# Two more tile pairs of a matrix product by seven products, two copies made independent, one load behind a wait, and a new order of all steps

## Chip, core and metric

The kernel runs on one core of a Trainium2 chip. The metric is the device time of one execution in microseconds; lower is better. The engines are TensorE (PE: matmuls and transposes into PSUM), VectorE (DVE) and ScalarE (ACT) for element-wise work, GpSimd (POOL), which here mostly issues the DMAs that convert float32 to float16, and SyncE (SP), which issues the other DMAs.

## What is computed

Local attention with eight global tokens, and then a low-rank mixer with a two-layer MLP. Shapes: q, k, v are 4 x 8 x 768 x 64 (batch, heads, tokens, head size), U is 768 x 32, V 32 x 768, w_ch1 512 x 2048, w_ch2 2048 x 512, all float32.

```python
scores = scale * np.matmul(q, k.transpose(0, 1, 3, 2))
keep = is_global | is_local            # key < 8, or 0 <= query - key < 96
scores = np.where(keep, scores + bias[None], -1e9)
a = np.exp(scores - np.max(scores, axis=-1, keepdims=True))
a = a / (np.sum(a, axis=-1, keepdims=True) + 1e-09)
x = np.matmul(a, v)                    # heads side by side: 4 x 768 x 512
h = x.transpose(0, 2, 1) @ U @ V
u = x + h.transpose(0, 2, 1)
out = u + np.maximum(u @ w_ch1, 0.0) @ w_ch2
```

## The kernel before

All arithmetic on TensorE is in float16 with float32 sums. The work is cut into small steps, each with a name, an engine and a Python function that issues its instructions. The list `ORDER` names all steps once. A planner walks through it, gives buffers and PSUM banks to the steps and a start time by its own estimates, and the program is issued in the order of these start times. So `ORDER` sets what each engine does after what; each engine works through its own instructions strictly in that order.

**Attention** goes by pairs of heads, 0 to 15, four pairs to a batch. A pair p has: loads of k, q and v (`lk`, `lq`, `lv`, by POOL, lines 457, 453 and 461; for pair 0, k and q come by SyncE in float32, line 471, and are cast by `Ck0`, `Cq0`); transposes of k and q on TensorE (`TK`, `TQ`) and copies out of PSUM (`EK`, `EQ`); a copy of the keys shifted by one block, with the global keys in its first 32 columns (`KO`, line 366 where SyncE makes it); the same for the values (below); scores (`S`, line 732, for batch 0 with a bias matmul `SB`, line 713), exponentials on ACT (`EX`, line 797), the mask product on DVE (`MK`), the product with the values (`PV`, lines 864 and 865), reciprocal and norm (`RC`, `NM`), a cast (`XC`), transposition and the product with U (`UP`, lines 838 and 843), copies and the product with V (`XE`, `XU`, `TE`, `HM`, line 964), and a copy of the result u into place (`E0`, `E1`). Which of ACT, DVE, SP or POOL makes a copy is a letter in a string of `CFG`, one letter for each pair: `KO`, `VO`, `XC`, `E`, `EK`, `EQ` and so on. `HR` says whether `HM` uses two groups of 64 rows (R) or all 128 rows (F).

**Shifted V.** `vo` holds V without its last block, and the global rows of V in its first 32 partitions for every block. `VC` copies all 128 partitions and `VG` then writes the 32 partitions over. With SyncE as their engine these are one DMA, a wait for its landing, and two more DMAs.

**MLP-1** (u @ w_ch1 with relu) has for each batch 16 tiles of 128 columns of w_ch1. An ordinary tile takes four 384-column matmuls for each half of the tokens, as one step with both halves (`M1a`, `M1b` and a relu `RL` of 768 columns, lines 1042 and 1060) or as two half tiles (line 1018, relus `RL` and `RM` of 384 columns, line 1024). `CFG["Z"]` names tile pairs (z and z + 8) of a batch that are computed together in the manner of Strassen and Winograd: seven products of two matmuls each (`ZP1` to `ZP7`, line 1113) in place of sixteen matmuls. They need sums of blocks of u (`ZT`, lines 1070 to 1073, once for a batch) and of w_ch1 (`ZS`, lines 1091 to 1094, kept in `zs` for pairs 4 to 7 and made in an `ep` buffer for others), copies of partial results out of PSUM on ACT (`ZU`, `ZW`, `ZX`), additions on DVE (`ZA`, `ZB`, `ZD`, line 1131) and relus (`ZR` on ACT, line 1164; `ZQ` and `ZV` on ACT, line 1170, or DVE, line 1172, by the strings `ZQ` and `ZR`).

**MLP-2** goes in three parts t of 128 + 128 tokens, all by seven products (`P1` to `P7`, eight matmuls each, line 1244) that need sums of the hidden values on DVE (`PA`, `PB`, lines 1197 to 1203) and of w_ch2 (`TWa`, `TWb`). A remainder step `RS` opens each part (line 1236) with products of `vs`. `DA` to `DG` add the products to the rows held in `x_sb` (lines 1256 and 1296), and `O` stores them (line 1311).

**Weights** come in four pieces each: `w1_0` to `w1_3` serve tile steps n = 0 to 3, 4 to 7, 8 to 11 and 12 to 15 of MLP-1 (the number after the dot in `M1a0.13` is n, the one before it the batch).

**The small V of the mixer** is loaded twice. POOL loads its two halves as float16 into `vs` (`vs0`, `vs1`); SyncE loads it whole in float32 into `vf`, a corner of `x_sb` (`mixl`, line 516), for `vs2`, the difference of the halves on DVE. The planner lets `mixl` depend on `back`, a memset of one element by DVE (line 532):

```python
uf = x_sb[1][:, 0, 0:NB * R].rearrange("p (c r) -> p c r", r=R)
vf = x_sb[1][0:R, 2:4].rearrange("p a b -> p (a b)")[:, 0:S]
```

The memset writes `uf`, the load writes `vf`, so nothing in the program makes the one wait for the other.

Of the kernel before, what the change touches and what calls it, by code (L numbers as in the profile page):

```python
# [32 lines left out]
M1a0.6 RL0.6 VC5 M1b0.7 MK5.0 M1a0.4 MK5.1 M1b0.10 RM0.10 TK6 EK6 KO6 VG5 M1b0.5 RM0.5 M1a0.0 M1c0.0 M1d0.0 M1b0.0  # L33
MK5.2 RM0.7 RL0.0 PA0.3 PV5 lq8 RL0.4 M1b0.8 RM0.8 lk8 mask6 M1a0.5 RL0.5 UP4 XE4 RC5 NM5 M1a0.12 lq9 PB0.3 XC5
M1a0.1 TWa0 M1a0.7 RL0.12 TWb0 M1b0.6 lv8 RM0.6 VC7 RL0.7 PA0.1 PB0.1 XU4 TE4 M1c0.1 lq10 M1d0.1 lk9 M1b0.1 RL0.1
PA0.0 lv6 M1a0.8 RL0.8 M1a0.9 lk10 RL0.9 M1b0.9 RM0.9 PB0.0 PA0.2 PB0.2 HM4 S7.0 EX7.0 MK7.0 RS0.0 E04 P20.0 TWa1
# [15 lines left out]
P61.1 TK14 EK14 DB1.0 P71.0 HM9 E09 DF1.1 RC11 NM11 DD1.0 S12.0 DC1.0 DB1.1 DC1.1 EX12.0 RS1.2 P11.2 P41.0 DA1.2
DG1.0 lk15 S12.1 EX12.2 P31.2 VC10 P71.1 VG10 EX12.1 MK10.0 MK10.2 PV10 TK13 EK13 KO13 MK12.0 XC11 UP11 DD1.1 RC10
KO14 XE11 NM10 XC10 P61.2 TQ13 EQ13 DB1.2 P21.2 DF1.2 UP10 XE10 P71.2 DD1.2 XU11 MK12.1 XU10 TE10 O1.3 P41.1 TE11
DG1.1 HM10 E010 S14.0 EX14.0 HM11 E011 E111 ZT2 P41.2 TD2 O1.1 ZP12.7 ZU2.7 S14.1 EX14.2 MK14.2 EX14.1 ZP12.6 ZU2.6
P51.2 DG1.2 DC1.2 O1.2 MK14.0 ZP22.7 TK15 M1b2.4 RM2.4 EK15 KO15 M1a2.1 TQ15 ZA2.7 ZP62.6 ZW2.6 M1b2.1 RL2.1 ZP62.7
ZW2.7 M1b2.5 ZP52.6 MK12.2 ZP72.6 EQ15 ZX2.6 ZB2.6 M1a2.5 RL2.5 ZP12.4 ZP42.6 ZR2.6 O1.5 M1a2.4 RL2.4 ZP32.6 M1a2.3
M1b2.3 ZD2.6 RM2.5 MK14.1 RL2.3 PV12 RC12 ZV2.6 ZP72.7 ZX2.7 ZP52.7 O1.4 O1.0 VG14 NM12 ZP22.6 M1a2.0 XC12 ZB2.7
M1b2.0 ZU2.4 ZV2.7 ZA2.6 ZP32.7 ZD2.7 RL2.0 PV14 ZP12.5 ZU2.5 RC14 NM14 PA2.0 ZP62.4 ZW2.4 UP12 ZP22.4 ZA2.4 ZP42.7
ZP62.5 XE12 ZW2.5 ZR2.7 ZP22.5 XU12 TE12 ZA2.5 M1a2.7 PB2.0 RL2.7 ZP72.4 ZP72.5 ZX2.5 ZP52.5 ZB2.5 HM12 ZV2.5 E012  # L60
ZP52.4 ZQ2.7 ZX2.4 M1a2.2 ZP42.5 ZR2.5 XC14 ZP32.5 UP14 XE14 ZB2.4 ZV2.4 ZP32.4 M1b2.2 RL2.2 ZD2.5 ZP42.4 ZR2.4 XU14
# [1335 lines left out]
```

## Time and profile before

| | us |
|---|---|
| median of 3 runs | 226.85 (224.6 to 227.18) |
| profiled execution | 227.05 |
| its span, first to last instruction | 225.3 |

The time of an execution is its span and 1.75 us around it. TensorE's granted clock is 1.00 all through. By stretch, from the profile's busy times (a stretch ends where TensorE begins the next kind of work, roughly):

| stretch (us) | what TensorE mainly does | PE busy | DVE busy | ACT busy | GB/s |
|---|---|---|---|---|---|
| 0 to 57.2 | attention and MLP-1 of batch 0 | 51.56 | 44.12 | 44.04 | 174 |
| 57.2 to 82 | MLP-2 of batch 0, attention of batch 1 | 24.80 | 20.80 | 15.98 | 140 |
| 82 to 109 | MLP-1 of batch 1 | 27.00 | 23.28 | 22.25 | 134 |
| 109 to 135 | MLP-2 of batch 1, attention of batch 2 | 26.00 | 21.60 | 16.36 | 60 |
| 160 to 182 | MLP-2 of batch 2, attention of batch 3 | 22.00 | 18.62 | 9.43 | 13 |
| 182 to 203 | MLP-1 of batch 3 | 21.00 | 16.57 | 15.55 | 76 |
| 203 to 225.2 | MLP-2 of batch 3, last stores | 18.92 | 16.03 | 1.36 | 73 |

Matmuls are pipelined: the busy time of a group of matmuls counts each from its start to its modelled end, and that is about twice the time after which the next one starts. What a matmul costs a full TensorE is read from the chain of waits, where several follow each other.

### The profile page before, as it was taken

Reading aid. Unit: us, or ns where it says so; the run is one execution under the profiler, and the core shown is the slowest. Engines: PE = TensorE matmul, PEld = TensorE weight load, DVE = VectorE, ACT = ScalarE, POOL = GpSimd, SP = SyncE. Lnnn points to the kernel's source line nnn. Section 1 sums busy time; section 2 is a strip of 40 time slices with the busy share of each in tenths; the row PEclk is TensorE's granted clock in tenths of the full one; section 3 lists DMA queues with packets and bytes.
Section 4 is the critical chain, followed back from the end, with each engine's and each line's share of the span. In section 5 each row is a group of like instructions: output and inputs, shape, how many; then the busy total and the mean of one; then the engine's idle time right before and its main releaser. Section 6 shows DMA issues by size and latency. Waiting matters only on the chain.

```text
span 225.3 us, 5972 instructions
## 1 busy us (share of the span) xinstructions
PE 216.3 (96%) x2422; PEld 157.7 (70%) x2422; DVE 181.5 (81%) x403; ACT 144.5 (64%) x257; POOL 72.5 (32%) x94
## 2 busy tenths in 40 slices
PE   7799889799999999999999999999999999999994
PEld 2556645566788976566788886666688876658883
DVE  5789847869978878788888879598987887979792
ACT  4898876688767659877665678778752357782000
POOL 8889956543794935010091000004000000000000
PEclk9999999999999999999999999999999999999999
DMA  6999999999999999874097501409200016000015
GB/s 173 172 167 141 178 181 177 188 196 167 160 130 127 144 151 219 151 121 80 8 95 48 129 2 51 145 4 102 70 11 3 0 49 235 1 0 4 23 57 202
DMA packets 87612, 24.01 MB, mean 107 GB/s; under 512 B 75840, under 2 KB 84736, under 8 KB 87584
## 3 DMA queue, kind: packets, MB, share of 16 engines
q0 software_dynamic: 71552, 13.93, 73.7%
q1 hardware_dynamic: 16032, 9.69, 15.4%
q8 instruction: 19, 0.31, 0.6%
q14 instruction: 9, 0.07, 0.1%
HBM read 27.56 MB, written 6.29 MB: 150 GB/s over the span
## 4 chain that ended last, share of the span: by engine, by line
PE 80%; DMA 15%; POOL 3%; issue 1%; ACT 0%; SPq 0%; DVE 0%; DVEq 0%; POOLq 0%
PE ps L1244 33%; PE ps L1113 14%; PE ps L1018 10%; DMA w<-in_moe_w_ch_dram 9%; PE ps L1042 7%; DMA vt<-in_v_dram 4%; PE ps L732 4%; PE ps L610 3%; PE ps L838 2%; DMA sA<-in_q_dram 2%; PE ps L865 2%; POOL stgq L457 2%; PE ps L864 1%; PE ps L964 1%; PE ps L1236 1%
## 5 line engine op out<-in xcount | busy, mean ns | idle before, releaser
L797 ACT ACTIVATE ep<-ps 128x1024 f16<-128x1024 f32 (+1 forms) x48 | 43.9, 951 | 16.0 <-PE ps L732 14.8
L1244 PEld LDWEIGHTS <-htr 128*128 128x128 f16 x392 | 36.3, 98 | 6.2 <-issue 2.2
L1018 PE MATMUL ps<-uT,w 128*128 128x384 f16 x176 | 33.2, 326 | 1.4 <-DMA w<-in_moe_w_ch_dram 1.4
L1256 DVE TENSOR_TENSOR x_sb<-x_sb,ps 128x256 f32<-128x256 f32 (+1 forms) x60 | 27.0, 466 | 9.3 <-PE ps L1244 9.0
L1244 PEld LDWEIGHTS <-sA 128*128 128x128 f16 x288 | 27.1, 98 | 4.1 <-issue 0.4
L1018 PEld LDWEIGHTS <-w 128*128 128x128 f16 x176 | 16.5, 98 | 12.2 <-DMA w<-in_moe_w_ch_dram 1.9
L1024 ACT ACTIVATE htr<-ps 128x384 f16<-128x384 f32 x44 | 20.4, 492 | 7.0 <-PE ps L1018 6.0
L1244 PE MATMUL ps<-w,sA 128*128 128x256 f16 x192 | 24.3, 273 | 0.0
L1244 PE MATMUL ps<-tB,htr 128*128 128x256 f16 (+1 forms) x200 | 23.9, 268 | 0.0
L457 POOL DMA_DIRECT2D stgq<-in_q_dram x24 | 20.2, 851 | 11.5 <-DMA w<-in_moe_w_ch_dram 5.8
L1244 PE MATMUL ps<-w,htr 128*128 128x256 f16 x192 | 23.8, 273 | 0.0
L457 POOL DMA_DIRECT2D stgk<-in_k_dram x24 | 20.3, 856 | 8.1 <-PE ps L610 5.2
L1042 PE MATMUL ps<-uT,w 128*128 128x384 f16 x112 | 21.3, 326 | 0.7 <-DMA w<-in_moe_w_ch_dram 0.7
L1131 DVE TENSOR_TENSOR htr<-ps,zu 128x384 f16<-128x384 f32 x30 | 16.5, 554 | 5.8 <-PE ps L1113 4.0
L461 POOL DMA_DIRECT2D vt<-in_v_dram x16 | 16.7, 1045 | 12.2 <-DMA vo<-vt 8.8
L810 DVE TENSOR_TENSOR ep<-ep,mask 128x1024 f16<-128x1024 f16 x24 | 16.2, 684 | 2.4 <-ACT ep L797 2.4
L362 ACT ACTIVATE zu<-ps 128x384 f32<-128x384 f32 x30 | 14.7, 495 | 5.0 <-PE ps L1113 4.0
L928 POOL DMA_DIRECT2D x<-x_sb x3 | 2.5, 823 | 46.2 <-DVE sA L1197 28.0
L1042 PEld LDWEIGHTS <-w 128*128 128x128 f16 x112 | 10.6, 98 | 7.5 <-DMA w<-in_moe_w_ch_dram 0.8
L903 DVE TENSOR_TENSOR x_sb<-ps,rcp 128x768 f32<-128x768 f32 x16 | 15.3, 957 | 0.5
L1113 PEld LDWEIGHTS <-w 128*128 128x128 f16 x108 | 10.1, 98 | 6.4 <-issue 0.2
L732 PE MATMUL ps<-qT,kT 64*128 64x128 f16 x192 | 14.1, 217 | 0.0
(125 smaller groups left out, 452.3 us busy)
## 6 DMA issues: line engine op xcount, KB each, us to landing
out_dram<-x_sb SPq DMA_DIRECT2D x22, 256.0 KB, 2.4
w<-in_moe_w_ch_dram POOLq DMA_DIRECT2D x8, 512.0 KB, 10.7
vt<-in_v_dram POOLq DMA_DIRECT2D x16, 192.0 KB, 6.4
stgk<-in_k_dram POOLq DMA_DIRECT2D x24, 96.0 KB, 5.8
stgq<-in_q_dram POOLq DMA_DIRECT2D x24, 96.0 KB, 5.7
...
```

Source lines behind the costliest of these rows:

```text
L457: nc.gpsimd.dma_start(o[:, i], src[b, h0 + i].rearrange("(n p) d -> p n d", p=P))
L461: nc.gpsimd.dma_start(vt[gv.slot][:, :, :, 0:D], v[b, h0:h0 + 2].rearrange("h (n p) d -> p h n d", p=P),)
L732: nc.tensor.matmul(t[:, hi, j * P:(j + 1) * P], lhs, qt[r, i * P:(i + 1) * P], start=not biased, stop=True, skip_group_check=biased,)
L797: nc.scalar.activation(ep[gep.slot][:, :, lo:512], ps[:, gsc.slot:gsc.slot + 2, lo:512], AF.Exp, scale=qk_scale)
L810: nc.vector.tensor_tensor(ev, ev, mv, ALU.mult)
L1018: nc.tensor.matmul(ps[:, g.slot, 0:HS], w1[:, dc, jt * P:(jt + 1) * P], ub[:, dc, i * HS:(i + 1) * HS], start=(dc == 0), stop=(dc == NDC - 1),
L1024: nc.scalar.activation(htr[:, jt, i * HS:(i + 1) * HS], ps[:, g.slot, 0:HS], AF.Relu)
L1042: nc.tensor.matmul(ps[:, g.slot + half, 0:HS], w1[:, dc, jt * P:(jt + 1) * P], ub[:, dc, half * HS:(half + 1) * HS], start=(dc == flat[0]) ...
L1113: nc.tensor.matmul(bank(g), a()[:, i], bq[:, i], start=first and i == 0, stop=last and i == 1, skip_group_check=True,)
L1131: return lambda: nc.vector.tensor_tensor(o, x(), y(), ALU.add)
L1244: nc.tensor.matmul(o if part is None else o[:, part], a[:, j, c0 + cols.start:c0 + cols.stop], bq[:, j] if part is None else bq[:, j, part ...
L1256: nc.vector.tensor_tensor(o, o, x, ALU.add)
```

## The change

- `Z` names pairs 2 and 3 for batch 2 too: six pairs instead of four there (batch 1 has four, batch 3 six), sixteen in all. Four ordinary tiles of batch 2 go (`M1` n = 2, 3, 6 and 7). The sums `ZS2.2` and `ZS2.3` are made in `ep` buffers.
- `VC` on SyncE copies partitions 32 to 127 only. `VG` then no longer waits for it; both wait for the load of V alone, and the product with the values waits for both.
- The memset `back` writes an element of `vf`. The load `mixl` writes the same place, and so is issued behind the memset.
- The four stores of rows 0 to 511 of batch 0 are split into halves by columns (`OS`).
- Many letters of the engine strings change, `HR` of pairs 2 and 3 from R to F, and the planner's size for `u16`.
- `ORDER` is new from end to end. Shown are its beginning before and after, up to the last piece of w_ch2, and the part around MLP-1 of batch 2 after.

```diff
-ones3 wz lk0 iota ones0 lk1 lq0 lq1 vz lk3 relf rel3 bias1 bias0 bias2 SB0.0 bias4 Ck0.1 Ck0.0 lv0 ones1 Cq0.0 vs1
-TK0 EK0.1 lk2 SB0.1 lq2 mask2 Cq0.1 EK0.0 TQ0 ones2 SB0.2 mask0 lq3 EQ0.0 lv1 EQ0.1 KO0.1 KO0.0 TK1 EK1 S0.2 TQ1 EQ1
-mask7 EX0.2 KO1 VC0 VG0 S0.0 EX0.0 S0.1 back EX0.1 TK3 EK3 SB1.2 KO3 lk4 u16 vs0 lv2 S1.2 EX1.2 SB1.1 S1.1 EX1.1 PV0
-RC0 NM0 TK2 EK2 SB2.2 KO2 XC0 TQ2 EQ2 VC1 VG1 lk5 SB1.0 S1.0 EX1.0 lv3 lq4 lq5 w1_0 w1_3 lk7 w1_2 SB2.1 S2.1 TQ3
-S2.2 EQ3 lq7 PV1 RC1 NM1 EX2.1 lv4 EX2.2 SB3.1 S3.1 EX3.1 UP0 XE0 SB2.0 mask1 XC1 S2.0 XU0 TE0 EX2.0 VC2 TK4 EK4 VG2
-SB3.0 S3.0 EX3.0 TK5 EK5 VC3 VG3 HM0 E00 SB3.2 S3.2 PV2 RC2 NM2 XC2 EX3.2 UP1 XE1 TQ4 PV3.0 PV3.1 PV3.2 RC3.2 EQ4
-lq6 w1_1 RC3.0 NH3.0 RC3.1 NH3.1 NH3.2 NM3 KO4 mixl XU1 lk6 TE1 lv5 TQ5 EQ5 UP2 XE2 HM1 E01 UP3.0 XU2 TE2 UP3.1
-UP3.2 XE3 HM2 XU3 E02 M1a0.3 M1c0.3 TE3 HM3 E13 E03 S4.1 KO5 EX4.2 w2_0 MK4.2 M1d0.3 M1b0.3 RL0.3 M1b0.13 EX4.1
-M1a0.14 MK4.1 RL0.14 TK7 M1a0.13 EK7 M1b0.14 ZS6 KO7 M1a0.2 RM0.14 M1c0.2 M1d0.2 TD0 M1b0.2 M1b0.15 TQ7 EQ7 RL0.13
-ZS5 VC4 VG4 RL0.2 RM0.15 S4.0 EX4.0 MK4.0 S5.0 EX5.0 M1a0.15 ZS7 M1a0.10 RL0.10 M1a0.11 RL0.11 M1b0.12 RL0.15
-M1b0.11 RM0.12 w2_2 RM0.13 RM0.11 TQ6 EQ6 w2_3 lv7 vs2 PV4 RC4 NM4 M1b0.4 mask3 XC4 RM0.4 w2_1 S5.1 EX5.1 EX5.2
...
+ones0 wz iota lk0 lq0 lk1 lq1 vz vs1 relf rel3 bias0 bias1 SB0.2 Ck0.0 lk3 SB0.1 lq2 Ck0.1 lv0 TK0 bias2 bias4 mask2
+mask1 lk2 Cq0.0 Cq0.1 TQ0 SB0.0 mask3 EQ0.0 EK0.0 KO0.0 EK0.1 KO0.1 lq3 ones1 ones3 lv1 EQ0.1 S0.0 TK1 EK1 KO1 ones2
+EX0.0 S0.2 EX0.2 S0.1 TQ1 EQ1 u16 lk5 mask0 SB1.2 TK3 EK3 KO3 lq5 VC0 VG0 lv2 EX0.1 lv3 vs0 SB1.1 w1_0 S1.2 EX1.2
+lk4 S1.1 EX1.1 TQ2 EQ2 lq4 SB1.0 S1.0 TK2 EK2 KO2 PV0 RC0 EX1.0 VC1 VG1 NM0 XC0 TQ3 lq7 w1_3 lk7 w1_2 EQ3 SB2.0
+SB2.2 S2.2 EX2.2 S2.0 EX2.0 PV1 RC1 NM1 XC1 SB2.1 S2.1 EX2.1 SB3.0 S3.0 EX3.0 UP0 XE0 VC2 VG2 VC3 SB3.1 S3.1 EX3.1
+XU0 TE0 VG3 SB3.2 lv5 S3.2 EX3.2 PV2 RC2 NM2 XC2 TK5 EK5 HM0 E00 lk6 PV3.0 PV3.1 PV3.2 RC3.1 RC3.0 NH3.0 UP1 XE1 UP2
+XE2 TQ5 RC3.2 EQ5 NH3.1 XU1 TE1 TK4 EK4 XU2 TE2 NH3.2 HM1 E01 UP3.0 UP3.1 UP3.2 XE3 NM3 HM2 E02 lv4 back mixl TQ4
+EQ4 w1_1 XU3 TE3 KO4 M1a0.3 TQ7 EQ7 M1c0.3 HM3 E03 KO5 E13 M1d0.3 S4.1 EX4.2 lq6 M1b0.3 RL0.3 M1b0.13 RM0.13 MK4.2
+M1b0.14 RM0.14 M1b0.15 RM0.15 EX4.1 TK7 EK7 KO7 M1b0.12 RM0.12 M1a0.15 ZS7 RL0.15 M1a0.13 M1a0.11 M1a0.2 w2_1 RL0.11
+S5.0 EX5.0 S4.0 ZS5 MK4.1 VC5 VG5 EX4.0 MK5.0 M1c0.2 w2_3 M1b0.9 M1a0.14 RL0.14 M1a0.12 ZS6 RL0.13 RM0.9 TD0 TK6 EK6
+M1d0.2 M1b0.2 RL0.2 M1a0.8 RL0.8 RL0.12 vs2 M1b0.11 RM0.11 VC4 VG4 w2_2 S5.1 EX5.1 M1b0.10 RM0.10 M1b0.5 EX5.2
+M1b0.6 RM0.6 w2_0 MK4.0 PV4 TQ6 RM0.5 M1a0.10 RL0.10 MK5.1 lk9 EQ6 M1a0.7 RC4 NM4 lq8 M1b0.7 RM0.7 KO6 M1a0.6 M1b0.4
...
+NM10 ZS2.2 P41.1 DG1.1 XC10 P21.2 UP10 XE11 XU11 P31.2 MK12.1 ZS2.3 XE10 XU10 TE10 ZP12.3 TE11 TQ13 ZU2.3 VC14 O1.4
+HM10 E010 TD2 DF1.2 HM11 P71.2 E111 O1.3 EQ13 VG14 S14.0 TK15 E011 EX14.0 O1.1 DD1.2 ZP12.2 ZU2.2 P51.2 P41.2 ZP22.3
+ZT2 EK15 DC1.2 DG1.2 ZA2.3 ZP62.2 ZW2.2 ZP62.3 ZW2.3 O1.2 ZP22.2 ZA2.2 MK12.2 TQ15 ZP72.2 ZX2.2 ZP72.3 ZX2.3 ZP52.2
+ZB2.2 ZV2.2 EQ15 O1.5 ZP52.3 ZB2.3 ZP42.2 ZR2.2 ZP42.3 ZR2.3 ZP32.2 ZD2.2 ZQ2.2 PV12 RC12 NM12 ZP32.3 ZD2.3 MK14.0
+S14.1 EX14.2 MK14.2 EX14.1 M1a2.5 ZP12.4 ZU2.4 MK14.1 ZQ2.3 ZP22.5 ZP12.5 ZU2.5 ZA2.5 M1a2.1 RL2.5 M1b2.1 RL2.1
+ZP62.4 PV14 ZV2.3 RC14 ZP62.5 NM14 ZW2.5 M1b2.5 ZP22.4 ZP72.5 XC12 UP12 ZP52.5 ZA2.4 ZP12.6 RM2.5 XE12 XU12 ZX2.5
+PA2.1 TE12 M1a2.4 ZP42.5 ZB2.5 ZV2.5 HM12 E012 ZU2.6 ZP62.6 ZW2.4 ZP72.4 ZR2.5 ZX2.4 RL2.4 ZP32.5 ZD2.5 ZW2.6 ZP22.6
+ZA2.6 ZP52.4 ZP52.6 ZB2.4 ZV2.4 ZP42.4 ZR2.4 ZQ2.5 ZP12.7 ZP72.6 ZP22.7 ZU2.7 XC14 ZA2.7 ZX2.6 ZB2.6 lv15 VG15
+ZP32.4 ZD2.4 UP14 ZP62.7 M1b2.4 KO15 XE14 XU14 ZW2.7 TE14 ZP32.6 ZP72.7 ZQ2.4 ZD2.6 RM2.4 ZQ2.6 ZP42.6 ZX2.7 ZR2.6
+ZP52.7 ZB2.7 ZV2.6 ZV2.7 M1a2.0 ZP42.7 ZP32.7 ZR2.7 PA2.2 ZD2.7 M1b2.0 ZQ2.7 PA2.3 HM14 RL2.0 PA2.0 RS2.1 P22.1
+P12.1 PB2.3 E014 S13.1 EX13.1 RS2.0 P12.0 EX13.2 DA2.0 P22.0 P52.1 PB2.2 S15.1 EX15.1 EX15.2 P52.0 P62.0 PB2.1 PB2.0
...
-    "NU": (0, 1, 2, 3, 4, 5, 6, 7, 8, 9, 10, 11, 12, 13, 14, 15), "back": "EK1", "early": 4, "att1": (0, 1, 2, 3, 4, 5, 6, 7), "att2": (0, 2, 4, 6), "mlp1": (7, 6, 5, 4, 3, 2, 1, 0), "mlp2": (6, 4, 2, 0), "Z": ((1, (4, 5, 6, 7)), (2, (4, 5, 6, 7)), (3, (2, 3, 4, 5, 6, 7))), "PA": "DDDDDDDDDDDDDDDD", "PB": "DDDDDDDDDDDDDDDD", "ZK": (4, 5, 6, 7), "ZE": {}, "AC": {}, "NZU": 4, "S1": ((0,), (1, 2)), "OS": (), "MH": {0: (4, 5, 6, 7, 8, 9, 10, 11, 12, 13, 14, 15), 1: (4, 5, 6, 7, 8, 9, 10, 11, 12, 13, 14, 15), 2: (4, 5, 6, 7, 8, 9, 10, 11, 12, 13, 14, 15), 3: (4, 5, 6, 7, 8, 9, 10, 11, 12, 13, 14, 15)}, "SD": {}, "KG": (), "BP": 4, "ZR": "DDDAADAD", "ZQ": "DDAADDDD", "TE": "DAADAAAAAAAAAAAA", "XE": "DAAAAAAAAADAAAAA", "EK": "ADADDDADAAAAAAAA", "EQ": "DDADAADDAAADDADD", "KO": "ADDDDDSDSSSSDAAD",
-    "HR": "FRRRRRRRFRRRFRRR", "IB": "AADD", "U16": "Q", "VS": "QQD", "C0": "DADADADA", "DL": (), "SPL": (0,), "BI": (0, 1, 2, 3), "EKS": "DDDADADA", "EQS": "DADADADA", "KOS": "DADADADA",
-    "VO": "DDDDDDDSSSSSASSS", "XC": "DDDDDAAADQDQAAQD", "E": "AAAAAADAAADAAAAA",
+    "NU": (0, 1, 2, 3, 4, 5, 6, 7, 8, 9, 10, 11, 12, 13, 14, 15), "back": "EK1", "early": 4, "att1": (0, 1, 2, 3, 4, 5, 6, 7), "att2": (0, 2, 4, 6), "mlp1": (7, 6, 5, 4, 3, 2, 1, 0), "mlp2": (6, 4, 2, 0), "Z": ((1, (4, 5, 6, 7)), (2, (2, 3, 4, 5, 6, 7)), (3, (2, 3, 4, 5, 6, 7))), "PA": "DDDDDDDDDDDDDDDD", "PB": "DDDDDDDDDDDDDDDD", "ZK": (4, 5, 6, 7), "ZE": {}, "AC": {}, "NZU": 4, "S1": ((0,), (1, 2)), "OS": ((0, 0), (0, 1), (0, 2), (0, 3)), "MH": {0: (4, 5, 6, 7, 8, 9, 10, 11, 12, 13, 14, 15), 1: (4, 5, 6, 7, 8, 9, 10, 11, 12, 13, 14, 15), 2: (4, 5, 6, 7, 8, 9, 10, 11, 12, 13, 14, 15), 3: (4, 5, 6, 7, 8, 9, 10, 11, 12, 13, 14, 15)}, "SD": {}, "KG": (), "BP": 4, "ZR": "DDDDDDAA", "ZQ": "DDADDDDD", "TE": "DDADAADAAAADDAAA", "XE": "DAAAAAAAAAAAADAA", "EK": "ADDDDADDAAADDAAA", "EQ": "DDAAAAADAAADAADA", "KO": "ADDDDDDDSSSSSSAS",
+    "HR": "FRFFRRRRFRRRFRRR", "IB": "AAAA", "U16": "Q", "VS": "QQD", "C0": "DDADDADA", "DL": (), "SPL": (0,), "BI": (0, 1, 2, 3), "EKS": "DDDADADA", "EQS": "AADADADA", "KOS": "DDDADADA",
+    "VO": "DDDDDDASSSSSDSSS", "XC": "DDDDDADADQAAQAQD", "E": "AAAAAAAAAAAADAAA",
...
@@ -529,11 +530,11 @@
                 (nc.gpsimd if e == POOL else nc.vector).tensor_tensor(o, v1, v2, ALU.subtract)
         return go
 
-    c_back = add(DVE, 0.07, lambda: nc.vector.memset(uf[0:1, 0, 0:1], 0.0), [c_bias[0]], name="back")
+    c_back = add(DVE, 0.07, lambda: nc.vector.memset((vf[0:1, 0:1] if uq else uf[0:1, 0, 0:1]), 0.0), [c_bias[0]], name="back")
     c_mixl = add(SP, 0.5 if uq else 1.1, load_mixer, [c_back], size=0.4 if uq else 2.3, parts=1 if uq else 2, name="mixl")
     if uq:
         c_u16 = add(
-            POOL, 0.84, lambda: nc.gpsimd.dma_start(u16[:, :, 0], moe_U.rearrange("(c p) r -> p c r", p=P)), size=0.8, name="u16",
+            POOL, 0.84, lambda: nc.gpsimd.dma_start(u16[:, :, 0], moe_U.rearrange("(c p) r -> p c r", p=P)), size=0.35, name="u16",
         )
     else:
         ue = ENG[CFG["U16"]]
@@ -681,7 +682,8 @@
         vm = ENG[CFG["VO"][p]]
 
         def vo_keys():
-            copy(vm, vo[gv.slot], vt[gv.slot][:, :, 0:NB - 1])
+            r = slice(GP if vm == SP else 0, P)
+            copy(vm, vo[gv.slot][r], vt[gv.slot][r, :, 0:NB - 1])
 
         def vo_globals():
             o, i = vo[gv.slot][0:GP], vt[gv.slot][0:GP, :, 0:1]
@@ -692,7 +694,7 @@
                 copy(vm, o, i.broadcast_to((GP, 2, NB - 1, DP)))
 
         VC = add(vm, {POOL: 0.75, DVE: 0.33, ACT: 0.75, SP: 0.1}[vm], vo_keys, [tv], size=0.5 if vm == SP else 0.0, fast=1, name=f"VC{p}")
-        VO = [add(vm, {POOL: 0.75, DVE: 0.33, ACT: 0.75, SP: 0.2}[vm], vo_globals, [VC], size=0.4 if vm == SP else 0.0, parts=2, fast=1, name=f"VG{p}")]
+        VO = [VC, add(vm, {POOL: 0.75, DVE: 0.33, ACT: 0.75, SP: 0.2}[vm], vo_globals, [tv] if vm == SP else [VC], size=0.4 if vm == SP else 0.0, parts=2, fast=1, name=f"VG{p}")]
 
         geps, MKs = [], []
```

More of the change, by code (lines that the diff above doesn't have):

```diff
@@ L32 @@
-M1b0.11 RM0.12 w2_2 RM0.13 RM0.11 TQ6 EQ6 w2_3 lv7 vs2 PV4 RC4 NM4 M1b0.4 mask3 XC4 RM0.4 w2_1 S5.1 EX5.1 EX5.2
[L33 to L36, printed above, removed]
@@ L52 @@
[L52 to L56, printed above, removed]
@@ L57 @@
[L57 to L61, printed above, removed]
@@ new lines @@
+M1d0.2 M1b0.2 RL0.2 M1a0.8 RL0.8 RL0.12 vs2 M1b0.11 RM0.11 VC4 VG4 w2_2 S5.1 EX5.1 M1b0.10 RM0.10 M1b0.5 EX5.2
+M1b0.6 RM0.6 w2_0 MK4.0 PV4 TQ6 RM0.5 M1a0.10 RL0.10 MK5.1 lk9 EQ6 M1a0.7 RC4 NM4 lq8 M1b0.7 RM0.7 KO6 M1a0.6 M1b0.4
+M1b0.8 RL0.7 XC4 UP4 RL0.6 M1a0.0 M1a0.1 M1c0.1 M1d0.1 M1b0.1 MK5.2 mask4 lk8 RM0.4 M1c0.0 M1d0.0 XE4 RM0.8 RL0.1
+lv6 PA0.3 PB0.3 mask7 M1b0.0 RL0.0 XU4 TE4 M1a0.5 PA0.1 PB0.1 PV5 RL0.5 M1a0.4 RL0.4 TWa1 M1a0.9 RS0.0 RC5 NM5 TWa0
+RL0.9 lk10 HM4 E04 S7.0 EX7.0 P20.0 P10.0 PA0.2 PB0.2 PA0.0 XC5 S6.1 EX6.2 RS0.1 P20.1 EX6.1 P10.1 TK8 PB0.0 lv7 TQ8
@@ L78 @@
+P73.1 DF3.1 O2.3 DF3.0 O3.0 P73.2 DF3.2 O3.1 O3.2a DG3.0 O3.3 DD3.1 P43.1 DD3.2 O3.5a DG3.1 O3.4 P43.2b P43.2a
+DG3.2b DG3.2a O3.5c O3.5b
 """.split()
 CFG = {
[L80 removed]
```

60 lines of the change are left out of this document (29 added, 31 removed).

## Prediction

> **What bounds the kernel now.** I began with the first lines of the page, engine by engine.
>
> ```profile
> span 225.3 us, 5972 instructions
> ...
> PE 216.3 (96%) x2422; PEld 157.7 (70%) x2422; DVE 181.5 (81%) x403; ACT 144.5 (64%) x257; POOL 72.5 (32%) x94
> ```
>
> TensorE (PE) lacks 9.0 us of the span. Where, the busy times by stretch say (start:end, length, busy time of PE, weight loads, DVE, ACT and POOL with instruction counts, granted clock, DMA share, GB/s):
>
> ```profile
> 25.20:45.00 19.80, 16.84 (x180) 10.40 (x181) 14.39 (x41) 14.02 (x26) 12.63 (x16) 1.00 1.70 185
> ...
> 57.20:222.00 164.80, 164.72 (x1788) 125.84 (x1787) 136.98 (x291) 100.44 (x181) 31.92 (x37) 1.00 0.65 83
> 122.00:135.00 13.00, 13.00 (x178) 10.90 (x176) 10.30 (x22) 8.79 (x16) 0.83 (x1) 1.00 0.26 57
> 135.00:160.00 25.00, 25.00 (x236) 16.31 (x234) 20.52 (x45) 19.51 (x40) 2.85 (x3) 1.00 0.48 76
> ```
>
> From 57.2 us, where MLP-2 of batch 0 begins, to 222 us PE lacks 0.08 us. After that comes a tail of some 3.3 us (last addition, last store), which the change leaves as it is. So what can be won lies in PE's own work, and before 57.2 us. There the waits of PE up to 45 us (line <- what it waited for: us in total, times, longest) name the cause:
>
> ```profile
> PE ps L1018 <- DMA w<-in_moe_w_ch_dram: 1.4, 2, 1.1
> ...
> PE ps L610 <- ACT stgq L362: 0.8, 1, 0.8
> PE ps L1042 <- DMA w<-in_moe_w_ch_dram: 0.7, 1, 0.7
> ```
>
> The chain of waits for the first 60 us (start, us, what) puts times to it:
>
> ```profile
> 1.25 4.46 DMA sA<-in_q_dram
> ...
> 21.97 9.37 DMA w<-in_moe_w_ch_dram
> ...
> 32.44 10.64 DMA w<-in_moe_w_ch_dram
> ...
> 55.26 1.95 PE ps L1018 x12
> ```
>
> PE waits for q of pair 0 until 5.71 us, for the fourth piece of w1 (w1_3) until 31.34 and for the second (w1_1) until 43.08; the first (w1_0) costs the 0.7 us of line 1042. The last line gives the true price of a 384-column matmul: 1.95/12 = 0.163 us.
>
> **The change, part by part**, against the profiled execution: 227.05 us, that is its span of 225.3 and 1.75 around it. It lies 0.2 above the median of 226.85.
>
> **Two more pairs by seven products.** In batch 2 the tile pairs 2 and 3 take 14 matmuls each instead of 16: 4 x 0.163 = 0.65 us less on PE, inside 57.2 to 222 us, where PE is full: **-0.65**. Against that DVE gets work, by these rows of the groups:
>
> ```profile
> L1131 DVE TENSOR_TENSOR htr<-ps,zu 128x384 f16<-128x384 f32 x30 | 16.5, 554 | 5.8 <-PE ps L1113 4.0 <-ACT zu L362 1.4
> ...
> L1091 DVE TENSOR_TENSOR zs<-w 128x256 f16<-128x256 f16 x4 | 1.1, 283 | 0.9 <-DMA w<-in_moe_w_ch_dram 0.9
> ```
>
> Six additions out of PSUM, 6 x 0.554 = 3.3 us; eight sums of w1 blocks (lines 1091 to 1094, 0.283 to 0.293), 2.3 us; the flat relus on DVE (0.35 for 768 columns, 0.25 for 384, line 1172), 0.35 + 2 x 0.25 = 0.85. Together 6.5 us. ACT loses the relus of the four tiles (2 x 0.81 in line 1060 and 4 x 0.49 in 1024: 3.6) and gets six copies, two relus and one flat relu (8 x 0.49 + 0.84 = 4.8): +1.2 us on 19.5 of 25. Does DVE have room? MLP-1 of batch 2 is the stretch 135 to 160: 20.52 of 25 busy. The new order puts the eight sums ahead of ZT2, in the stretch before (2.7 us free of 13). Moved between engines in this stretch: E012 and TE12 come to DVE (some 0.9 and 0.3), EQ15, KO15 go (0.55, 0.42), relus balance: +0.2. So 20.5 + 3.3 + 0.85 + 0.2 = 24.9 us of DVE work in a stretch of 24.35. PE first needs nearly all of it at the first P5 (line 1244) of MLP-2. The new order puts four products of 0.87 us, a score step of 0.55 and two remainder steps of 0.22 between the last MLP-1 matmul and that one (4.5 us), and three of the four PB steps behind it. I take the cover as just sufficient: 0, with +0.5 to +2.9 (all 27.2 us in the stretch) if it is gone.
>
> **The load order.** w1_0 moves ahead of k and q of pair 4: two loads of 192 KB at 185 GB/s (the stretch 25 to 45) are 2.1 us. It was waited for by 0.7, and the last step of the attention before it frees PE at about the same time: -0.7. w1_3 gets q of pair 7 in front (+1.04): PE stood idle for it briefly and would do so longer, less the 0.33 us of pair 7's transposes that now run ahead: +0.65. w1_1 gets k of 6 and v of 5 for q of 6 (+1.04) and V's load (96 KB, +0.5): it lands at about 44.7. But the order has more for PE first: from M1b0.13 (first user of w1_3) to the first user of w1_1 I count 15 half tiles of 0.65, three score steps (0.89) and two transposes of 0.33, 11.3 us; before it was 9.8. 32.4 + 11.3 + 0.5 of small gaps = 44.2: PE waits 0.5 instead of 1.3: -0.8. Sum **-0.85**; bounds -2.1 (no wait for w1 left) and +2.1 (each of the two later pieces costs its full delay). The last w2 piece has v of pair 7 no longer before it (-1.04) and V's load instead (+0.5), so it lands no later than now.
>
> **V's small load.** SyncE now issues it (0.46 us) behind a memset of DVE, which the order has near 27 us. Out of the first 6 us go 96 KB of some 1 MB (173 GB/s in the first slice): q of pair 0, on the chain until 5.71, can land up to 0.55 earlier. Only part survives to 57 us, as w1 paces what follows: **-0.2** (bounds 0 and -0.55). Its one user is vs2, needed by the first remainder step at 57.6 us. Behind the waiting SyncE stand only copies of K and V after 48 us.
>
> **SyncE's copies.** The rows of the DMA issues before:
>
> ```profile
> x_sb<-in_moe_V_dram SPq DMA_DIRECT2D x1, 96.0 KB, 4.8
> ...
> vo<-vt SPq DMA_DIRECT2D x16, 20.6 KB, 2.0
> ```
>
> The keys' copy (165 KB, 3.1 us) and the two copies of global rows go out together instead of one after the other: about 3 us less to a PV, for which PE nowhere waits after 45 us. 0, and 0 if the cover goes, since the path only gets shorter. Two more K copies and four split stores add some eight issues to SyncE (0.46 to 0.66 each). The splits stand between copies for batch 2 at 80 to 105 us; without PE's cover they would cost up to 4 x 0.6 = 2.4 us. I take 0, as batch 1's MLP lies between.
>
> **Row groups and engines.** The low-rank step of pairs 2 and 3 runs with 128 rows: 2 x 0.325 for 2 x 0.17, +0.3 us of PE in a stretch with 2.96 us idle: **+0.1**. Some 35 small copies change between DVE and ACT; with the 6.5 above DVE ends about 5.5 us up, ACT equal. Where PE is full they cost nothing so long as it stays full.
>
> **Sum**: -0.65 - 0.85 - 0.2 + 0.1 = -1.6, so 225.45 for an execution like the profiled one. A new order of all 1135 steps will not hit every time as planned, while there is only 0.08 us for it to win after 57.2: I add 0.3. Less the 0.2 to the median: **225.6 us**.
>
> **Rivals.**
> *DVE becomes the bound in batch 2* (slower). For it: 24.9 to 27.2 us of work for 24.35, and DVE waited 5.8 us in line 1131 for PE or ACT, idle time that it can't make up. Against: at 135 to 160 it still had 4.5 us, and the PBs are put off. It decides once DVE's backlog at the first P5 exceeds the 4.5 us of PE work put between. Price 0.5 to 2.9, up to all 6.7 added if its waits grow as well: 226.85 - 0.65 + 0.8 to 6.7 = 227 to 233, likeliest 228.5. The Trainium skill (Perfetto Trace Analysis, Identifying the Most-Contended Engine) says that matmul busy time is no good measure and that weight-load share is; by that DVE (81%) is the most contended engine here and not TensorE (70%), and the change would load the wrong one. The trace speaks against it from 57.2 us on: matmuls follow each other at their streaming price, without a wait.
>
> *The loads fit as planned.* No PE wait for w1 (2.1), V's load out of the start (0.55), up to 0.9 more of the idle time before 45 us: 226.85 - 0.65 - 2.65 to 3.5 = 222.7 to 223.6. Against: each w1 piece but the first is queued later.
>
> *Nothing is won at the start*: the wait only moves from w1_0 and w1_1 to w1_3. 226.85 - 0.65 = 226.2.
>
> **Chances.** Forecast (224.2 to 226.0) 0.43; DVE bound 0.22; loads fit 0.15; nothing at the start 0.11; a stall or gain of the new order that I don't see 0.09, half each way. 2% is about what a measurement of this kernel can tell from no change: 222.3 and 231.4. Below lie 0.05 of the loads' rival and 0.04 of the unseen: 0.09. Above lie 0.08 of DVE's and 0.04: 0.12. Leaving out 0.09 below and 0.11 above gives the range, 222.4 to 230.0.
>
> **What would show it.** PE's first matmul of line 1236 with remainder terms near 56.5 instead of 57.6; PE waits for w1 near 1.5 us in sum, the longest at 31 to 33; some 2418 matmuls; DVE busy near 187 us and no PE wait in line 1244 around 155 to 165. Wrong: PE waits on DVE there (first rival), or PE busy in the long stretch more than 1 us below its length.

## The result, and the profile after

| | median, us | range, us | executions |
|---|---|---|---|
| before | 225.19 | 224.1 to 228.5 | 20 |
| changed | 223.84 | 223.2 to 224.34 | 20 |

The ratio is 0.9935, with a 95% interval of 0.9914 to 0.9955: a gain of 1.35 us in medians, clear of zero and far within the 2% that were called no change. The profiled execution of the changed kernel took 223.47 us, 0.4 below its median; that of before (227.05) lies 1.9 above the 225.19 of the table. The two profiles therefore differ by 3.6 us where the kernels differ by 1.35. So I took one more profiled execution of the unchanged kernel, called the second before below (224.93 us).

The first lines of the changed kernel's page, a group of part 5 (the DVE additions out of PSUM, line 1131 before) and the row of SyncE's larger copies of V:

```profile
span 221.7 us, 6001 instructions
...
PE 215.8 (97%) x2423; PEld 158.7 (72%) x2423; DVE 187.7 (85%) x422; ACT 143.6 (65%) x254; POOL 71.9 (32%) x94
...
L1133 DVE TENSOR_TENSOR htr<-ps,zu 128x384 f16<-128x384 f32 x36 | 19.1, 552 | 2.1 <-PE ps L1115 1.6
...
vo<-vt SPq DMA_DIRECT2D x8, 123.8 KB, 3.2
```

DVE does 6.2 us more, yet the span is shorter, and the additions (36 instead of 30) stood idle for 2.1 us where they did for 5.8. In the changed file the lines lie one or two further down: the remainder step is 1238, MLP-2's products 1246, MLP-1 1020 and 1044.

Busy times by stretch of the changed kernel (start:end, length, busy time of PE, weight loads, DVE, ACT, POOL, clock, DMA share, GB/s):

```profile
0.00:10.00 10.00, 8.80 (x90) 4.74 (x90) 7.40 (x26) 8.16 (x15) 9.18 (x21) 1.00 1.00 171
25.00:45.00 20.00, 19.77 (x212) 13.03 (x209) 15.44 (x43) 17.00 (x31) 13.95 (x18) 1.00 1.69 190
45.00:57.00 12.00, 12.00 (x129) 8.14 (x128) 11.14 (x23) 9.59 (x19) 6.65 (x8) 1.00 1.86 179
...
122.00:135.00 13.00, 13.00 (x169) 10.66 (x168) 11.33 (x30) 8.93 (x16) 0.00 (x0) 1.00 0.59 123
135.00:160.00 25.00, 25.00 (x251) 16.60 (x250) 22.81 (x48) 19.79 (x40) 2.66 (x3) 1.00 0.43 60
```

PE lacks 0.23 us from 25 to 45 us (before: 2.96 from 25.2), and it is full in the two stretches of batch 2 that got the added DVE work. All waits of PE in the changed kernel, and then those of the second before (line <- what it waited for: us in total, times, longest):

```profile
PE ps L1347 <- POOL zero L380: 0.9, 1, 0.9
PE ps L866 <- DVE vo L365: 0.5, 1, 0.5
PE ps L592 <- DMA stgk<-in_k_dram: 0.4, 1, 0.4
PE ps L734 <- ACT qT L363: 0.3, 1, 0.3
```

```profile
PE ps L1345 <- POOL zero L379: 0.9, 1, 0.9
PE ps L591 <- DMA stgk<-in_k_dram: 0.9, 1, 0.9
PE ps L610 <- ACT mask L1331: 0.5, 1, 0.5
PE ps L838 <- DVE x L364: 0.3, 1, 0.3
PE ps L591 <- DMA stgq<-in_q_dram: 0.2, 1, 0.2
PE ps L964 <- ACT tmp L362: 0.2, 1, 0.2
```

Neither has a wait for w1. The 2.1 us of them in the first profile, on which the prediction worked, are not there in an execution near the median. Seven of the twenty executions of before took over 226 us and none of the changed kernel over 224.34; whether the late ones all wait for w1, no profile shows. The chain of the changed kernel (start, us, what) shows the price of a 384-column matmul as before, 1.95/12 = 0.163 us, and MLP-1's run starting without a transfer ahead of it:

```profile
27.89 0.33 PE ps L1044 x2
...
30.52 1.95 PE ps L1020 x12
```

The first remainder step opens MLP-2 of batch 0. The matmuls of that line, with the first and last start at the end (min/median/max ns ahead of them), in the first before, the second before and the changed kernel:

```profile
L1236 PE MATMUL ps<-tmp,vs x36: 269/269/280, 57.5 to 203.2; 64*128 64x256 f16 x36
```

```profile
L1236 PE MATMUL ps<-tmp,vs x36: 269/269/280, 55.3 to 201.1; 64*128 64x256 f16 x36
```

```profile
L1238 PE MATMUL ps<-tmp,vs x36: 269/269/280, 54.0 to 199.7; 64*128 64x256 f16 x36
```

From that start to the end of the span: 225.3 - 57.5 = 167.8, 223.2 - 55.3 = 167.9 and 221.7 - 54.0 = 167.7. Two executions of one kernel differ by 2.2 us ahead of this mark and by 0.1 behind it. In all eleven profiled executions that have the work of one of the two kernels behind the mark, this stretch is 167.6 to 167.9. The mark splits all that follows.

The 167.7 still holds the saving of 0.65, since the new order moves other work behind the mark: by the counts of matmuls, six of the scores and one low-rank step on two row groups, some 0.2 and 0.17 us (an estimate from the start-to-start times in the chain). -0.65 + 0.37 is -0.3, and the trace has -0.2. Ahead of the mark the second before and the changed kernel differ by 1.3, of which these 0.37 are moved work.

### The profile page after: what moved, and what is told of

Same layout as the page of the kernel before. It is cut to its first block, busy times and chain, and to the rows that moved or that the text cites. A ratio compares the mean times of both kernels' runs of the same rounds, so it can differ in the third digit from the quotient of the medians.

```text
span 221.7 us, 6001 instructions
## 1 busy us (share of the span) xinstructions
PE 215.8 (97%) x2423; PEld 158.7 (72%) x2423; DVE 187.7 (85%) x422; ACT 143.6 (65%) x254; POOL 71.9 (32%) x94
## 4 chain that ended last, share of the span: by engine, by line
PE 92%; DMA 4%; DVE 2%; POOL 0%; issue 0%; ACT 0%; DVEq 0%; POOLq 0%
PE ps L1246 34%; PE ps L1115 17%; PE ps L1020 12%; PE ps L1044 7%; PE ps L734 5%; PE ps L611 4%; DMA vt<-in_v_dram 4%; PE ps L840 3%; PE ps L867 2%; PE ps L866 2%; PE ps L715 2%; PE ps L966 2%; PE ps L1238 1%; PE ps L1347 1%; DVE x_sb L905 1%; PE ps L845 1%
## 5 line engine op out<-in xcount | busy, mean ns | idle before, releaser
L1246 PEld LDWEIGHTS <-sA 128*128 128x128 f16 x288 | 27.3, 98 | 4.2 <-issue 0.7
L1020 PE MATMUL ps<-uT,w 128*128 128x384 f16 x160 | 29.8, 326 | 0.0
L1246 PE MATMUL ps<-w,sA 128*128 128x256 f16 x192 | 23.8, 273 | 0.0
L1246 PE MATMUL ps<-w,htr 128*128 128x256 f16 x192 | 23.2, 273 | 0.0
L1020 PEld LDWEIGHTS <-w 128*128 128x128 f16 x160 | 15.1, 98 | 9.4
L1026 ACT ACTIVATE htr<-ps 128x384 f16<-128x384 f32 x40 | 18.7, 501 | 3.8 <-PE ps L1020 3.5
L1133 DVE TENSOR_TENSOR htr<-ps,zu 128x384 f16<-128x384 f32 x36 | 19.1, 552 | 2.1 <-PE ps L1115 1.6
L363 ACT ACTIVATE zu<-ps 128x384 f32<-128x384 f32 x36 | 16.7, 492 | 4.7 <-PE ps L1115 3.3
L1044 PE MATMUL ps<-uT,w 128*128 128x384 f16 x96 | 18.9, 326 | 0.0
L1115 PEld LDWEIGHTS <-w 128*128 128x128 f16 x120 | 11.4, 98 | 7.0
L1115 PE MATMUL ps<-uT,w 128*128 128x384 f16 x64 | 15.0, 326 | 0.0
L867 PEld LDWEIGHTS <-ep 128*128 128x128 f16 x192 | 12.6, 97 | 1.9 <-issue 0.8
```

Of the source, the lines that this page charges most:

```text
L867: nc.tensor.matmul(o, e[:, hi, (j + 1) * P:(j + 2) * P], vv[:, hi, i, 0:D1], start=(i == 0), stop=True)
L1020: nc.tensor.matmul(ps[:, g.slot, 0:HS], w1[:, dc, jt * P:(jt + 1) * P], ub[:, dc, i * HS:(i + 1) * HS], start=(dc == 0), stop=(dc == NDC - 1),
L1026: nc.scalar.activation(htr[:, jt, i * HS:(i + 1) * HS], ps[:, g.slot, 0:HS], AF.Relu)
L1044: nc.tensor.matmul(ps[:, g.slot + half, 0:HS], w1[:, dc, jt * P:(jt + 1) * P], ub[:, dc, half * HS:(half + 1) * HS], start=(dc == flat[0]) ...
L1115: nc.tensor.matmul(bank(g), a()[:, i], bq[:, i], start=first and i == 0, stop=last and i == 1, skip_group_check=True,)
L1133: return lambda: nc.vector.tensor_tensor(o, x(), y(), ALU.add)
```

## The experiments

Times are medians beside executions of the kernel before on the same chip (224.98, 224.92 and 225.02 us in the three groups); "over the mark" is the time from the first remainder step to the end.

**1. The first piece of w1 later.** In the changed kernel's `ORDER`, `w1_0` and `w1_3` stand side by side behind the loads of pair 4:

```diff
- vs0 SB1.1 w1_0 S1.2 EX1.2 lk4 ... EQ2 lq4 ... TQ3 lq7 w1_3 lk7
+ vs0 SB1.1 S1.2 EX1.2 lk4 ... EQ2 lq4 w1_0 w1_3 ... TQ3 lq7 lk7
```

> The changed kernel with the first and fourth piece of w1 next to each other and behind k and q of pair 4, as in the kernel before; nothing else moved. In the profile of before the first piece landed 4.5 us after the load in front of it and waits for w1 cost PE 2.1 us, in that of the changed kernel 2.5 us and nothing. Theory 1 (the loads): the first piece lands at 27 to 29 us instead of 23.8, PE waits for it by 0.5 to 1.5 us, the time is 224.4 to 225.4. Theory 2 (matmuls and chance): 223.6 to 224.0.

Measured: 227.78, ratio 1.0126 (1.0083 to 1.017), 3.9 us above the changed kernel and outside both theories. w1_0 landed at 26.62 instead of 23.79, but PE didn't wait for it. Its longest wait:

```profile
PE ps L610 <- DMA stgq<-in_q_dram: 2.3, 1, 2.3
```

It waits for q of pair 7, which now comes behind two weight pieces while its transposes (`TQ7`) still stand early in PE's order. In the profiled execution the mark lies at 56.7, 2.7 later than in the changed kernel. That execution took 226.18 us, at a mean granted clock of 0.999. The other five took 227.46 to 229.46 at 0.985 to 0.998, so a part of the 3.9 us goes with a lower clock, of which no profile was taken. To see whether that wait was the price, the next kernel keeps these loads and moves only `TQ7 EQ7`, from behind `M1a0.3` to behind `RM0.15`:

```diff
- KO4 M1a0.3 TQ7 EQ7 M1c0.3 ... M1b0.15 RM0.15 EX4.1
+ KO4 M1a0.3 M1c0.3 ... M1b0.15 RM0.15 TQ7 EQ7 EX4.1
```

> The changed kernel with the first and fourth piece of w1 behind k and q of pair 4, as in the run that came out at 227.78, and besides the transposes of q of pair 7 behind three more half tiles on PE. That run's profile had PE waiting 2.3 us for q of pair 7. If that one wait was its whole cost: 223.6 to 224.4, and no PE wait of more than 0.7 us between 28 and 45 us. If the place of the first piece of w1 costs by itself: 224.8 to 226.

Measured: 224.42, ratio 0.9981 (0.9957 to 1.0005). Of the 3.9 us 3.4 went with two steps moved. The rest lies just above the first theory and below the second: 0.6 us over the changed kernel in medians, 1.0 by the ratios, whose intervals don't overlap. So the place of these loads costs something by itself as well. In the profiled execution (224.95 us, mark at 55.5) PE has one wait between 28 and 45 us:

```profile
PE ps L610 <- DMA stgk<-in_k_dram: 0.5, 1, 0.5
```

It is for k of pair 7, which comes behind the two weight pieces too. Besides, the planner issues 26 filler matmuls on `zero` for this order, not 19, and four of them (0.34 us) stand inside MLP-1. The runs don't separate the two. The larger cost was a load that PE's in-order queue asks for before it has come.

**2. An extra load ahead of w1_1.** Two transfers of 96 KB, q of pair 15 into a place nobody reads, in the kernel before and in the changed one:

```diff
+            if i == 1:
+                o = sA[:, 2, 0:2].rearrange("p a b -> p (a b)").rearrange("p (n h d) -> p h n d", n=NB, h=2)
+                for j in range(2):
+                    nc.gpsimd.dma_start(o[:, j], q[3, 6 + j].rearrange("(n p) d -> p n d", p=P))
```

> The kernel before with one load more ahead of the second piece of w1: two more DMAs of 96 KB (q of pair 15) into a place that nothing reads until later. Such a load takes 1.25 us of the queue. In the second profile of before (224.93 us) the pieces of w1 and w2 land 0.16 to 0.3 us before PE needs them (w1_1 at 40.85, used at 41.01). Theory (the order before has no slack to the loads): 0.9 to 1.3 us slower, 225.9 to 226.3. Rival (loads are hidden, what comes late in slow executions is something else): below 0.4 us.

> The same load more in the changed kernel, ahead of the second piece of w1. There this piece lands at 40.55 and is first used near 42.0, the last piece of w2 at 52.05 and is used at 55. Theory (the new order has slack there): 0 to 0.4 us slower, 223.8 to 224.3. Rival (both orders are equally tight): 0.9 to 1.3 us slower, as in the kernel before.

Measured: 226.27 in the kernel before, ratio 1.0039 (1.0015 to 1.0064), so +0.9 by the ratio and +1.25 in medians; 224.06 in the changed kernel, 0.2 over its 223.84 from another group. PE's waits in the kernel before with the load:

```profile
PE ps L598 <- DMA stgk<-in_k_dram: 1.6, 1, 1.6
PE ps L1025 <- DMA w<-in_moe_w_ch_dram: 1.3, 1, 1.3
```

The 1.6 lies in the first 20 us, ahead of the extra load; the 1.3 is for w1_1.

And in the changed kernel with it:

```profile
PE ps L1027 <- DMA w<-in_moe_w_ch_dram: 0.7, 1, 0.7
```

That 0.7 stands at 31.6 us, for w1_3, ahead of the extra load (issued at 31.8), so it is not the load's doing; it does show that the changed kernel can wait for w1 as well. In the second before, w1_1 lands at 40.85 and is used at 41.01, and the last piece of w2 lands at 56.26 and is used at 56.5: no wait, and no room. In the changed kernel w1_1 lands at 40.55 and is used at about 42.0, w2 at 52.05 for 54.0. The new order wins slack here.

**3. The products alone.** Changed kernel, pairs 2 and 3 of batch 2 as ordinary tiles again, at the places of their products:

```diff
-"Z": ((1, (4, 5, 6, 7)), (2, (2, 3, 4, 5, 6, 7)), (3, (2, 3, 4, 5, 6, 7)))
+"Z": ((1, (4, 5, 6, 7)), (2, (4, 5, 6, 7)), (3, (2, 3, 4, 5, 6, 7)))
```

> The changed kernel with pairs 2 and 3 of batch 2 as ordinary tiles again, put where their products stood. PE gets 0.65 us of matmuls more in a stretch without a wait, DVE 6.5 us less. Theory 1 (PE full from 57 us on, so each matmul counts): 224.3 to 224.8, ratio to before about 0.9965. Rival (DVE was as tight as PE there, and what the products gave was lost to it): 223.2 to 223.9.

Measured: 224.66, ratio 0.9982 (0.9957 to 1.0008): 0.8 over the changed kernel. The span and the mark of its profiled execution:

```profile
span 222.7 us, 5986 instructions
```

```profile
L1236 PE MATMUL ps<-tmp,vs x36: 269/269/280, 54.3 to 200.6; 64*128 64x256 f16 x36
```

Over the mark 222.7 - 54.3 = 168.4, against 167.7: the two pairs are worth 0.7 there, against the 0.65 of four matmuls. Without them the interval of the ratio takes in 1: in medians these runs don't tell the rest of the change from nothing.

**4. More work for DVE in batch 2.** Changed kernel, with one or two more additions behind each of the six `ZB`, on a buffer that is free there and that a memset fills first:

```diff
+            def with_more(f=tt(quad(z + hj, 1), w_, u3)):
+                f()
+                for _ in range(2 if b == 2 else 0):
+                    nc.vector.tensor_tensor(early[:, 0:768], early[:, 0:768], early[:, 0:768], ALU.add)
```

> The changed kernel with more work for DVE in MLP-1 of batch 2: two additions of 128x768 float16 into an unused buffer after each of the six second additions there (ZB), and one memset, 12 x 0.55 + 0.3 = 6.9 us. Between 135 and 160 us DVE was busy for 22.8 of 25. If the cover that the prediction named is just sufficient: 2 to 4 us longer, with PE waits in the products of MLP-2 of batch 2. If DVE has ample room there: below 0.5 us longer. The output does not change.

> The changed kernel with one addition more on DVE after each of the six ZB of batch 2 and the memset: 6 x 0.55 + 0.3 = 3.6 us. With 6.9 us the time rose by some 3.4, so DVE had about 3.5 us left there. If that cover is one block: 0 to 0.5 us slower, 223.8 to 224.3. If DVE's work counts in part wherever it stands: half of the larger run, 1.5 to 1.9 us. The output does not change.

Measured: with two, 227.21, ratio 1.0117 (1.0089 to 1.0144); with one (`1 if b == 2`), 224.53, ratio 0.9981 (0.9957 to 1.0004), between the two theories. Waits of PE with two:

```profile
PE ps L1117 <- DVE htr L1135: 1.0, 3, 0.5
...
PE ps L734 <- DVE htr L1135: 0.7, 1, 0.7
```

The expectation looked for waits in the products of MLP-2. Only 0.2 us are found there (line 1253); the others stand in the products of MLP-1 and in a score step. The mark, with two (span 225.6 us) and then with one (span 223.1 us):

```profile
L1245 PE MATMUL ps<-tmp,vs x36: 269/269/280, 54.2 to 203.5; 64*128 64x256 f16 x36
```

```profile
L1245 PE MATMUL ps<-tmp,vs x36: 269/269/280, 54.6 to 201.1; 64*128 64x256 f16 x36
```

In these traces an added addition takes 0.55 us and the memset 0.38: 12 x 0.55 + 0.38 = 7.0 us and 6 x 0.55 + 0.38 = 3.7 us. Over the mark the two kernels take 171.4 and 168.5, that is 3.7 and 0.8 more than the changed kernel. So 7.0 - 3.7 = 3.3 and 3.7 - 0.8 = 2.9 us were free. Back to back, an added addition is followed by the next start after 0.47 to 0.58 us; counted so, the added work is 6.7 and 3.2 us, and 3.0 and 2.4 were free. Some 2.5 to 3 us more for DVE are free here, and beyond that each costs about its own time.

**5. Four small parts.** V's small load at once again in the changed kernel, by the memset of before; and, the other way about, the new memset in the kernel before:

```diff
-lambda: nc.vector.memset((vf[0:1, 0:1] if uq else uf[0:1, 0, 0:1]), 0.0)
+lambda: nc.vector.memset(uf[0:1, 0, 0:1], 0.0)
```

> The changed kernel with V's small load again issued at once (the memset writes the other place). The profile of the changed kernel has q of pair 0 landing at 5.1 us and that of before at 5.7. Theory 1 (the gain lies in the loads ahead of the first remainder step, and V's load out of the first 6 us is part of it): q lands at 5.6 to 5.8 again, the first remainder step comes 0.3 to 0.6 us later than 54.0, the time is 224.1 to 224.5 against 223.84. Theory 2 (the gain is the 0.65 us of matmuls and a chance difference between the two profiled executions): no difference, 223.6 to 224.0.

> The kernel before with V's small load behind the memset, nothing else. With it in the changed kernel undone the time did not move (223.83 against 223.84). Theory 1 (the order before has no slack to the loads, so 0.5 us of loads count there): q of pair 0 lands 0.3 to 0.6 us earlier and the time falls by 0.2 to 0.6 us, to 224.5 to 224.9. Rival (it is hidden in both): 225.0 to 225.3.

Measured: 223.83, ratio 0.9952 (0.9928 to 0.9976), and 225.48, ratio 1.0008 (0.9972 to 1.0043): no difference that these runs resolve, and the second interval leaves room for 0.6 us less and 1.0 more. In the first, q of pair 0 came at 5.61 instead of 5.11, and PE waited 0.9 us for its cast where it hadn't before; the mark came at 54.4 in one execution, and the median didn't move. In the second, q came at 4.93 instead of 5.71 and 5.48. The half microsecond is there in the landing. That other waits before the mark swallow it fits the unmoved median, but isn't shown.

V's copies one behind the other again, over all 128 partitions (and `VC`, `VG` exchanged in `ORDER` where the new one has `VG` first):

```diff
-            r = slice(GP if vm == SP else 0, P)
-            copy(vm, vo[gv.slot][r], vt[gv.slot][r, :, 0:NB - 1])
+            copy(vm, vo[gv.slot], vt[gv.slot][:, :, 0:NB - 1])
...
-        VO = [VC, add(vm, ..., vo_globals, [tv] if vm == SP else [VC], ...
+        VO = [VC, add(vm, ..., vo_globals, [VC], ...
```

> The changed kernel with SyncE's copies of shifted V in a row again: all 128 partitions, wait, then the global rows. Theory 1 (no PE wait hangs on them): 223.6 to 224.1, no difference to the changed kernel. Rival (the new order relies on the shorter path): products with the values of pairs 7 to 15 wait, 0.3 to 2.5 us slower, with a PE wait at line 866 or 867 naming these copies.

Measured: 223.87, ratio 0.9958 (0.9936 to 0.9981). In medians that is the changed kernel's time, so no wait hangs on these copies that the median shows.

The low-rank steps of pairs 2 and 3 on two row groups again:

```diff
-"HR": "FRFFRRRRFRRRFRRR"
+"HR": "FRRRRRRRFRRRFRRR"
```

> The changed kernel with the low-rank step of pairs 2 and 3 by two groups of 64 rows again, as before. Each step is 0.325 us of PE with 128 rows and 0.17 with groups. If PE is full from 25 us on, as the profile of the changed kernel has it (19.77 of 20 us busy from 25 to 45): 0.2 to 0.3 us faster, 223.5 to 223.7. If the loads still set the pace there: no difference.

Measured: 224.15, ratio 0.9963 (0.994 to 0.9985). Taking back the dearer form wins nothing; the 0.3 us above the changed kernel can't be told from zero, as the intervals overlap.

The split stores, the letters of the engine strings and the size of `u16` weren't undone one by one.

**6. The kernel before once more**, unchanged, for a second profile:

> The kernel before, unchanged, profiled once more. The first profile was of an execution of 227.05 us, 1.9 above the median of 225.19. Theory 1a (the waits for w1 seen there are the rule): PE waits for w1 sum to 1.5 us or more, the first remainder step at 57 to 58 us. Theory 1b (the loads come late in some executions only, and those are the slow ones): an execution near 225 us has waits for w1 below 0.7 us and the first remainder step at 55 to 56 us; from there to the end of the span it takes the same 167.8 us.

Measured: 224.93, with the waits and the mark shown in the result. Its busy times up to 25 us, and then those of the changed kernel from 10 us (its first 10 are in the result):

```profile
0.00:10.00 10.00, 7.42 (x55) 3.59 (x57) 6.44 (x22) 5.31 (x12) 7.91 (x19) 1.00 1.03 172
10.00:25.00 15.00, 15.00 (x286) 9.90 (x280) 12.83 (x31) 13.72 (x18) 14.34 (x18) 1.00 1.94 152
```

```profile
10.00:25.00 15.00, 13.79 (x263) 9.50 (x262) 12.99 (x31) 11.81 (x15) 13.16 (x17) 1.00 2.07 167
```

PE is busy 1.4 us more in the changed kernel's first 10 us, but 1.2 us less in the 15 behind them: up to 25 us the two are about level (22.59 and 22.42). The first MLP-1 matmul comes at 28.7 us in the second before and at 27.7 in the changed kernel. Below them a third row, from the kernel before with V's small load behind the memset (experiment 5), is shown:

```profile
L1042 PE MATMUL ps<-uT,w x112: 324/326/337, 28.7 to 187.6; 128*128 128x384 f16 x112
```

```profile
L1044 PE MATMUL ps<-uT,w x96: 322/326/337, 27.7 to 188.1; 128*128 128x384 f16 x96
```

```profile
L1042 PE MATMUL ps<-uT,w x112: 324/326/336, 27.6 to 187.2; 128*128 128x384 f16 x112
```

So this start scatters by as much as the two kernels differ. It lies at 28.8, 28.7 and 27.6 in three executions with the order of before and no extra load, and at 27.2 to 28.4 in eight with the changed order of these loads (the changed kernel and experiments 2 to 5). From it to the mark, six of the eight take 26.3 us; the other two have waits for w1 of 0.4 and 0.7 and take 27.0 and 27.2. The three with the order of before take 28.7, 26.6 and 27.3, with waits for w1 of 2.1, 0 and 0.4. Without such waits, and without the 0.37 us of moved work, both orders take about the same time there.

None of these kernels beats the changed one; the two that equal it (223.83 and 223.87) undo a part that has no effect on the median.

## Why the prediction was right, and where it was not

**The bound** was read rightly. PE is full from the first remainder step on, with 167.7 to 167.9 us in both kernels, so that only matmuls saved there, or time ahead of that mark, change the result.

**The two more pairs** were forecast at -0.65 and measured at -0.7 over the mark, -0.8 in medians. This is the part whose cause is shown.

**DVE's cover** was taken as just sufficient, with 24.9 us of work for 24.35. It is sufficient with some 2.5 to 3 us to spare: 22.81 busy of 25 there, no wait of PE on DVE. My count put 4.4 us more into that stretch, each operation at its duration; 2.3 more are found there (20.52 before), 1.0 in the 13 us ahead of it and 0.9 in the 22 us behind it, where 18.62 became 19.50. (With the windows set by the mark instead, the 2.3 is 2.1.) So the rival with DVE as the bound fell, but its kind is real: it needs that much more, and experiment 4 shows what it then looks like. The Trainium skill (Perfetto Trace Analysis, Identifying the Most-Contended Engine) judges TensorE's headroom by its share of peak matmul work and by its weight-load share; only the second was worked out here, and by it DVE is the more contended engine (85% against 72% now). Here the traces decide against that: 3.7 us more on DVE cost 0.8, and 0.65 us of matmuls less paid in full.

**The load order**, -0.85 in the forecast, is the step with a wrong reason. It was worked out from 2.1 us of waits for w1 in one late execution; the second before has none, and a third execution with that order (experiment 5, V's small load late) 0.4. The landing of w1_1 was put at 44.7 and came at 40.55: I had started from the late landing (43.08) of a late execution, and added the loads moved ahead at 185 GB/s. One of its sums is off as well, by little: 1.04 less 0.33 is 0.71, not 0.65. The forecast wait of 1.5 us for w1 is nil in the changed kernel's profile. The rival "the loads fit as planned" has this part right, but it priced the missing waits at 2.1 us, from the same profile, and came out too low (222.7 to 223.6). What the new order did win ahead of the mark is 1.3 us against the second before, 0.37 of it moved work. 1.0 of the 1.3 are there when MLP-1 begins, but experiment 6 shows that this start scatters as much under either order. In experiment 1 some 0.6 to 1.0 us go when the places of w1_0 and w1_3 are undone and `TQ7` is moved along, so these places are likely a part of it; but 0.34 us of that is filler, and the wait found is for k of pair 7 and not for w1. How the gain ahead of the mark divides among the moves stays open. The landing of POOL's first load of k scatters between 6.4 and 8.7 us in the executions profiled here, so that a single pair of profiles can't tell.

**V's small load** (-0.2) and the **row groups** (+0.1) have no effect that these runs resolve. Both fall ahead of the mark, where PE still has gaps; that the gaps hide them is likely and not shown, and 0.1 to 0.2 us are less than medians of these runs can tell apart. **SyncE's copies** were forecast at 0 and are 0. The 0.3 added for a new order that misses somewhere behind 57 us wasn't needed; nothing new is late there. The sign of some 2418 matmuls came out as 2423, and the five more are filler on `zero` (19 against 14).

**The total**: 225.6 against 223.84. As a ratio to the median then known the forecast said 0.9945, and 0.9935 (0.9914 to 0.9955) was measured. Most of the distance in microseconds is the kernel before itself, 226.85 in three executions and 225.19 in twenty. That the ratio came out so near is in part luck: half of the forecast gain is the two pairs and was right for its reason, and the other half was priced by waits that an execution near the median doesn't have. The mark was expected near 56.5 from 57.5 and came at 54.0: 1.3 of that 2.5 too early is ahead of the second before, the rest is that execution.
